# Two raw weight buffers instead of eight, 15 places for split tiles instead of 12, and a newly planned expert stage

## The chip, the cores and the metric

The kernel runs on one core of a Trainium2 chip. The metric is the device time of one execution in microseconds, as the median over runs. Its engines run their own instruction streams and wait for each other through semaphores: PE is the matrix engine (TensorE), ACT the scalar engine, DVE the vector engine, POOL is GpSimd, and SP does nothing but issue DMAs and read registers here. Every time below is from the times of the kernel before or from one profiled execution of it.

## The reference

A causal attention with a window and sink tokens is followed by a mixture of experts, in which each token goes to one expert by the order of its logits, and each expert takes at most 384 tokens.

```python
B, H, S, D = (4, 8, 768, 64); n_sink, window = (4, 128)
keep = is_sink | in_window                       # in_window: 0 <= row - column < 128
a = softmax(where(keep, q @ k.T / sqrt(D), -1e9)); attn = a @ v
x = attn.transpose(0, 2, 1, 3).reshape(B * S, H * D)          # 3072 tokens x 512
N, D, E, F = (3072, 512, 8, 1024)
cap = N // E                                                  # 384
logits = x @ w_gate
for idx in argsort(-logits.flatten()):                        # greedy: the best pairs first
    tok, e = idx // E, idx % E
    if assigned[tok] >= 0 or counts[e] >= cap: continue
    assigned[tok] = e; counts[e] += 1
for e in range(E):
    h = maximum(x[assigned == e] @ w1[e], 0)
    out[assigned == e] = h @ w2[e]
```

All is in float32.

## The kernel before

The attention runs first, in 24 chunks of 128 rows; its result goes to `x_dram` in device memory and the logits stay on chip. The change touches nothing of it.

The experts follow in eight rounds, k = 0 to 7. A round finds by vector work and small matmuls (`phase`, called routing here) the expert that fills up next and its 384 tokens, as the register value `ei` and three columns of row numbers `idx`. The routing of the next round goes on between the matmuls of the round before, on DVE and PE (lines L500 to L672; `cmp` at L500 and L503 are its large comparisons on DVE, `pr` at L519 the matmuls that count them).

A round then has these tasks:

- **Weights** (`weights`). SP reads the expert's number (L676) and issues eight loads of 512 KB (L691): tiles j = 0 to 3 are quarters of `w1`, 4 to 7 quarters of `w2`. A load fills one place of the ring `raw`, which has `NR` places. Each tile is split for exact float32 products: ACT rounds it to `wh` (L693), then DVE takes `wl` as `raw` minus `wh` (L695). `wh` and `wl` are rings of `NW` places. So a load waits until DVE has split the tile that was loaded `NR` loads earlier, and a split waits until PE has read the tile that was split `NW` splits earlier.
- **Rows** (`rows`). POOL issues three gathers of 128 token rows each from `x_dram` into `xg0` to `xg2` (L700). PE transposes them (L708), ACT rounds the result to `xh` (L710) and DVE makes the rest `xl` (L711).
- **Layers** (`mlp`). Layer 1 has eight groups of 12 matmuls into `ph` (L724; for the first two groups of round 0 L721 and L729), after each of which ACT makes `hh` (L731) and DVE `hl` (L732). Layer 2 has three tiles of 24 matmuls into `py` (L740), each of which ACT copies to `yo` (L743) and POOL scatters to the output (L745).

In round 0 the rows are wanted first, and a task named `rowed` on SP holds the loads from j = 2 on (L681): SP reads a word of the tile `xg2`, and so waits until that gather has landed.

Nothing of this order is written by hand. Each task is added to a `Graph` with its engine, a cost, and what it reads and writes; `Graph.order` is a list scheduler that plays the engines forward in time, with a latency for each pair of engines (`ML`), a bias for each class of tasks (`BIAS`), and a window (`WIN`) within which the task of the highest rank is taken though another could start earlier. The program is then emitted in that order on every engine, and each engine executes its instructions in order. The costs decide the order alone, not what an instruction takes on the chip. `run` also puts small matmuls into idle stretches of PE before the first expert matmul (`warm`, L562).

Of the kernel before, what the change touches and what calls it, by code (L numbers as in the profile page):

```python
# [244 lines left out]
def schedule(cfg,off,T,nb=NC,dl={}):
    o=table(cfg); bf=buffers(cfg); WIN=cfg['win']
    rdeps=collections.defaultdict(list); nd={}; ready={}
# [54 lines left out]
    while len(out)<total:  # L302
        best=None
        for e,a in avail.items():
# [67 lines left out]
def plan():  # L372
# [7 lines left out]

RUN=[(4,0)]*2+[(2,2)]*6
STEPS=[(26,64),(20,64),(15,32),(10,32),(5,32),(0,32)]
ML={'VV':127,'EV':200,'EA':220,'VE':300,'AE':260,'AV':142,'VA':130,'AP':180,'PV':180,'PE':215,'VP':180,'PA':180,'PP':60,'AA':35,'EE':0,
    'VS':900,'SD':1500,'VD':1700,'PD':1250,'AD':1700,'ED':1250,'DA':900,'DV':900,'DP':900,'DE':1600,'DD':0,'EP':220,'PQ':1560,}

GWAIT=2000
class Graph:

    def __init__(self): self.t=[]; self.lw={}; self.rd={}
    def add(self,e,cost,fn,r=(),w=(),name='',cls='',lat=None):  # L390
        i=len(self.t); dep={}
# [14 lines left out]
    def order(self,bias,win,free):  # L406
# [12 lines left out]
        while len(out)<n:  # L419
            best=None  # L420
            for e,a in av.items():
# [4 lines left out]
                if e=='D':  # L426
                    W=[(i,max(te,ready[i])) for i in a if T[i][4][0]=='L']; Q=[(ready[i],i) for i in a if T[i][4][0]!='L']
                    i=min(W)[0] if W else None
                    if Q:
                        r,j=min(Q)  # L430
                        if i is None or (max(te,r)<max(te,ready[i]) or max(te,r)==max(te,ready[i]) and max(te,r)>=r+GWAIT-1): i=j
                    x=(0,max(te,ready[i]),i)
# [18 lines left out]
class Moe:  # L451
# [98 lines left out]
    def pools(self,ctx,w1,w2,x_dram,out):  # L550
        tc=self.tc; self.w1,self.w2,self.x_dram,self.out=w1,w2,x_dram,out
        sb=ctx.enter_context(tc.tile_pool(name="fsb",bufs=1)); ps=ctx.enter_context(tc.tile_pool(name="fps",bufs=1,space=PSUM))
        def ring(n,shape,dt,name,p=sb): return [p.tile(shape,dt,name=f"{name}{j}") for j in range(n)]
        self.NR=8; self.raw=ring(self.NR,[128,1024],F32,"raw"); self.NW=12
        self.wh=ring(self.NW,[128,1024],F32R,"wh"); self.wl=ring(self.NW,[128,1024],F32R,"wl")
        self.xg=ring(3,[128,DM],F32,"xg"); self.xh=ring(2,[128,4,CAP],F32R,"xh"); self.xl=ring(2,[128,4,CAP],F32R,"xl")
        self.hh=ring(1,[128,8,CAP],F32R,"hh")[0]; self.hl=ring(1,[128,8,CAP],F32R,"hl")[0]; self.yo=ring(3,[128,DM],F32,"yo")
        self.pt=ring(2,[128,512],F32,"pt",ps); self.ph=ring(3,[128,512],F32,"ph",ps); self.py=ring(2,[128,512],F32,"py",ps); self.pr=ring(1,[128,512],F32,"pr",ps)
        self.nr=0; self.regs={}; self.sc_=[]
# [114 lines left out]
    def weights(self,g,k):  # L674
        nc=self.nc
        def load(): self.regs[k]=nc.sync.value_load(self.ei[k][0:1,0:1],min_val=0,max_val=E-1)  # L676
        g.add('S',100,load,[f'ei{k}'],[f'reg{k}'],f'reg{k}',f'L{k}')
        for j in range(8):
            if k==0 and j==2:

                g.add('S',100,lambda: nc.sync.value_load(self.xg[2][0:1,0:1].bitcast(I32)),['xg2'],['rowed'],'rowed','L0')  # L681
            n=8*k+j; q=n%self.NR; raw=self.raw[q]; s=n%self.NW; wh,wl=self.wh[s],self.wl[s]
            def ld(j=j,raw=raw):
                ei=self.regs[k]
                if j<4:
                    src=self.w1[bass.ds(ei,1),:,256*j:256*j+256].rearrange("o (d p) f -> p (o d) f",p=128)
                    dst=raw.rearrange("p (d f) -> p d f",d=4)
                else:
                    src=self.w2[bass.ds(ei,1),256*(j-4):256*(j-4)+256,:].rearrange("o (f p) d -> p (o f) d",p=128)
                    dst=raw.rearrange("p (f d) -> p f d",f=2)  # L690
                nc.sync.dma_start(dst,src)  # L691
            g.add('D',1450,ld,[f'reg{k}']+(['rowed'] if k==0 and j>1 else []),[f'raw{q}'],f'L{k}.{j}',f'L{k}')
            g.add('A',947,lambda wh=wh,raw=raw: nc.scalar.activation(wh,raw,AF.Copy),[f'raw{q}'],[f'wh{s}'],f'H{k}.{j}',f'W{k}')  # L693
            e='V' if (k,j) in LOV else 'P'
            g.add(e,{'V':1160,'P':2303}[e],lambda wh=wh,wl=wl,raw=raw,e=e: (nc.vector if e=='V' else nc.gpsimd).tensor_tensor(wl,raw,wh.bitcast(F32),OP.subtract),  # L695
                  [f'raw{q}',f'wh{s}'],[f'wl{s}'],f'W{k}.{j}',f'W{k}')
    def rows(self,g,k):
        nc=self.nc; idx=self.idx[k]; b=k%2
        for t in range(3):
            g.add('P',1350,lambda t=t: nc.gpsimd.indirect_dma_start(out=self.xg[t],out_offset=None,in_=self.x_dram,in_offset=bass.IndirectOffsetOnAxis(ap=idx[:,t:t+1],axis=0)),  # L700
                  [f'idx{k}'],[f'xgi{t}',f'xg{t}'],f'G{k}.{t}',f'G{k}')
            g.add('D',1250,None,[f'xgi{t}'],[f'xg{t}'],f'g{k}.{t}',f'G{k}',lat=700)
        for c in range(4):

            tp,tn=(self.py[c%2],f'py{c%2}') if k==0 and c>1 else (self.pt[c%2],f'pt{c%2}')
            pts=[tn,tn+'.1',tn+'.2']
            for t in range(3):
                g.add('E',92,lambda t=t,c=c,tp=tp: nc.tensor.transpose(tp[:,128*t:128*t+128],self.xg[t][:,128*c:128*c+128],self.idn),  # L708
                      [f'xg{t}'],[pts[t]],f'X{k}.{c}.{t}',f'X{k}')
            g.add('A',371,lambda c=c,tp=tp: nc.scalar.activation(self.xh[b][:,c,:],tp[:,0:CAP],AF.Copy),pts,[f'xh{b}.{c}'],f'xh{k}.{c}',f'X{k}')  # L710
            g.add('V',469,lambda c=c,tp=tp: nc.vector.tensor_tensor(self.xl[b][:,c,:],tp[:,0:CAP],self.xh[b][:,c,:].bitcast(F32),OP.subtract),pts+[f'xh{b}.{c}'],[f'xl{b}.{c}'],f'xl{k}.{c}',f'X{k}')  # L711
# [38 lines left out]
    def graph(self):  # L750
        g=Graph()
        for k in range(E):
            self.phase(g,k)
            if k==0: self.rows(g,k); self.weights(g,k); self.mlp(g,k)
            else: self.weights(g,k); self.rows(g,k); self.mlp(g,k)
        return g
    def run(self):
        g=self.graph(); self.g=g
        o=g.order(BIAS,WIN,{})
        self.o=o  # L760
# [11 lines left out]
LOP=[]  # L772
LOV=[(k,j) for k in range(E) for j in range(8) if (k,j) not in LOP]
WARM=[2, 2, 2, 1, 1, 1, 3]
WIN=[0, 666753, 5574]
BIAS={'G0': 6671635, 'G1': 6449503, 'G2': 6705779, 'G3': 8034144, 'G4': 7734947, 'G5': 6407711, 'G6': 6446165, 'G7': 7529680, 'H0': 7140392, 'H1': 6230422, 'H2': 7467794, 'H3': 7341794, 'H4': 8337522, 'H5': 6670993, 'H6': 7528230, 'H7': 8147223, 'L0': 6671635, 'L1': 7366959, 'L2': 8033333, 'L3': 6450452, 'L4': 8157017, 'L5': 7375597, 'L6': 7318303, 'L7': 6494864, 'M0': 7584506, 'M1': 6454307, 'M2': 6446111, 'M3': 5919116, 'M4': 5072608, 'M5': 7410515, 'M6': 7280220, 'M7': 6416193, 'R0': 7765513, 'R1': 8337522, 'R2': 7898561, 'R3': 8766281, 'R4': 7977893, 'R5': 7316483, 'R6': 7567827, 'R7': 7411586, 'T0': 6409393, 'T1': 8034144, 'T2': 6412879, 'T3': 7184173, 'T4': 7399728, 'T5': 7511516, 'T6': 6689144, 'W0': 8310018, 'W1': 7084371, 'W2': 6099157, 'W3': 6473218, 'W4': 6419299, 'W5': 6298013, 'W6': 8117911, 'W7': 6494864, 'X0': 5238855, 'X1': 7198893, 'X2': 6446165, 'X3': 7313265, 'X4': 5911130, 'X5': 5797303, 'X6': 8357941, 'X7': 7271989, 'Y0': 6444567, 'Y1': 7966386, 'Y2': 6670239, 'Y3': 7243724, 'Y4': 8658080, 'Y5': 7230830, 'Y6': 6666651, 'Y7': 7710047}

def attention_general(ctx,tc,qd,kd,vd,iwd,ident,idn,x_dram,L,n_sink,window):

# [91 lines left out]
```

## Time and profile before

| what | value |
|---|---|
| median of 3 runs | 489.02 us (488.76 to 491.45) |
| profiled execution, its own time | 490.33 us |
| its span, first to last instruction | 488.5 us |
| granted TensorE clock, mean | 0.973 |
| attention | 0 to 138.07 us |
| routing and rows of round 0 | 138.07 to 168.69 us |
| expert rounds | 168.69 to 482.50 us |
| PE busy in the expert rounds | 300.72 of 313.81 us |

The time of an execution is about 1.8 us longer than its span. An engine's busy time counts its own work and not the issue of DMAs; what it waited for is taken from the semaphore that came last. "SPq" and "POOLq" are the instruction queues of those engines. L12 is line 12 of the kernel before. In the changed kernel the same lines stand one lower (up to L677) or two lower (L691 is L693, L700 is L702, L740 is L742).

### The profile page before, as it was taken

Reading aid. Unit: us, or ns where it says so; the run is one execution under the profiler, and the core shown is the slowest. Engines: PE = TensorE matmul, PEld = TensorE weight load, DVE = VectorE, ACT = ScalarE, POOL = GpSimd, SP = SyncE. Lnnn points to the kernel's source line nnn. Section 1 sums busy time; section 2 is a strip of 40 time slices with the busy share of each in tenths; the row PEclk is TensorE's granted clock in tenths of the full one; section 3 lists DMA queues with packets and bytes.
Section 4 is the critical chain, followed back from the end, with each engine's and each line's share of the span. In section 5 each row is a group of like instructions: output and inputs, shape, how many; then the busy total and the mean of one; then the engine's idle time right before and its main releaser. Section 6 shows DMA issues by size and latency. Waiting matters only on the chain. (4 is left out here: it accounts for less than half of the span.)

```text
span 488.5 us, 14325 instructions
## 1 busy us (share of the span) xinstructions
PE 442.8 (91%) x5570; PEld 364.5 (75%) x5570; DVE 377.9 (77%) x1167; ACT 226.6 (46%) x667; POOL 171.8 (35%) x322
## 2 busy tenths in 40 slices
PE   8799999999754979989999989989999998999994
PEld 4577777777632668768878868868978877988983
DVE  5899999999956977988987998898898869531210
ACT  4987888888300361541452451262272167332110
POOL 5887878877710300420330230041053023201001
PEclk9999999999965899999999999999999999999998
DMA  8766766753210560930940750571291299301001
GB/s 265 247 222 187 229 217 203 228 171 105 75 43 18 167 228 1 325 148 1 306 147 23 234 215 28 168 264 45 87 323 43 74 355 371 108 0 66 0 22 44
DMA packets 44453, 73.28 MB, mean 150 GB/s; under 512 B 3425, under 2 KB 20961, under 8 KB 44385
## 3 DMA queue, kind: packets, MB, share of 16 engines
q1 hardware_dynamic: 39968, 59.11, 36.5%
q0 software_dynamic: 3840, 12.59, 7.2%
q8 instruction: 44, 0.72, 0.6%
q10 hardware_dynamic: 576, 0.67, 0.5%
q14 instruction: 25, 0.20, 0.1%
HBM read 59.77 MB, written 12.58 MB: 148 GB/s over the span
## 5 line engine op out<-in xcount | busy, mean ns | idle before, releaser
L693 ACT ACTIVATE wh<-raw 128x1024 fp32r<-128x1024 f32 x64 | 67.6, 1060 | 71.6 <-DMA raw<-w 36.7
L700 POOL DMA_INDIRECT xg<-x_dram,idx x24 | 34.7, 1444 | 164.1 <-issue 49.1
L724 PE MATMUL ph<-xh,wh 128*128 128x384 f32 x248 | 87.8, 354 | 0.2 <-DVE hl L732 0.2
L695 DVE TENSOR_TENSOR wl<-raw,wh 128x1024 fp32r<-128x1024 f32 x64 | 77.8, 1219 | 12.1 <-ACT wh L693 11.4
L724 PE MATMUL ph<-xh,wl 128*128 128x384 f32 x248 | 83.7, 337 | 0.0
L724 PE MATMUL ph<-xl,wh 128*128 128x384 f32 x248 | 83.5, 337 | 0.0
L731 ACT ACTIVATE hh<-ph 128x384 fp32r<-128x384 f32 x64 | 31.2, 488 | 106.5 <-PE ph L724 94.4
L740 PE MATMUL py<-wh,hh 128*128 128x512 f32 x192 | 78.6, 409 | 2.2 <-ACT yo L743 1.8
L740 PE MATMUL py<-wh,hl 128*128 128x512 f32 x192 | 75.6, 394 | 1.6 <-DVE hl L732 1.6
L24 ACT ACTIVATE P<-pp,nmx 128x128 f32<-128x128 f32 x192 | 68.7, 381 | 15.7 <-DVE nmx L97 14.7
L740 PE MATMUL py<-wl,hh 128*128 128x512 f32 x192 | 75.3, 392 | 0.0
L745 POOL DMA_INDIRECT out<-yo,idx x24 | 31.9, 1331 | 114.1 <-ACT yo L743 73.6
L732 DVE SCALAR_TENSOR_TENSOR hl<-ph,hh 128x384 fp32r<-128x384 f32 x64 | 35.4, 555 | 27.9 <-ACT hh L731 27.4
L724 PEld LDWEIGHTS ph<-xh,wh 128*128 128x128 f32 x248 | 46.9, 189 | 2.2 <-DVE hl L732 0.6
L724 PEld LDWEIGHTS ph<-xl,wh 128*128 128x128 f32 x248 | 46.7, 188 | 1.7
L724 PEld LDWEIGHTS ph<-xh,wl 128*128 128x128 f32 x248 | 46.6, 188 | 0.0
L83 PE MATMUL pp<-kk,q 64*64 64x204 f32 (+2 forms) x768 | 42.9, 330 | 3.0 <-ACT P L24 1.7
L740 PEld LDWEIGHTS py<-wh,hl 128*128 128x128 f32 x192 | 36.0, 188 | 10.7 <-DVE hl L732 2.8
L740 PEld LDWEIGHTS py<-wh,hh 128*128 128x128 f32 x192 | 36.1, 188 | 9.5 <-ACT yo L743 2.8
L24 ACT ACTIVATION_READ_ACCUMULATOR P<-pp,nmx 128x1 f32 x192 | 41.9, 218 | 0.0
L118 POOL TENSOR_TENSOR E<-PT,me 128x256 f32<-128x256 f32 x48 | 35.4, 755 | 12.5 <-ACT PT L24 12.5
L740 PEld LDWEIGHTS py<-wl,hh 128*128 128x128 f32 x192 | 36.2, 188 | 4.6
(166 smaller groups left out, 799.5 us busy)
## 6 DMA issues: line engine op xcount, KB each, us to landing
raw<-w SPq DMA_DIRECT2D x64, 512.0 KB
kk<-kd SPq DMA_DIRECT2D x23, 272.0 KB
v<-vd SPq DMA_DIRECT2D x24, 256.0 KB
x_dram<-xt SPq DMA_DIRECT2D x24, 256.0 KB
q<-qd SPq DMA_DIRECT2D x22, 256.0 KB
xg<-x_dram,idx POOLq DMA_INDIRECT x24
out<-yo,idx POOLq DMA_INDIRECT x24
us<-ud SPq DMA_DIRECT2D x1, 288.0 KB
```

Source lines behind the costliest of these rows:

```text
L24: def act(*a,**k): last[:]=[nc.scalar.activation(*a,**k)]
L83: PE.matmul(sp[o,s,204*u+a:204*u+204],q[p,2*g+u,o],kk[p,2*i-2+f+a//68:2*i+f+1,2*g+u],start=True,stop=True)
L118: def op_A(c,g): G.tensor_tensor(T('E',c)[:,2*g:2*g+2],diag(c,g),me[:,None].to_broadcast([128,2,2,64]),OP.mult)
L693: g.add('A',947,lambda wh=wh,raw=raw: nc.scalar.activation(wh,raw,AF.Copy),[f'raw{q}'],[f'wh{s}'],f'H{k}.{j}',f'W{k}')
L695: g.add(e,{'V':1160,'P':2303}[e],lambda wh=wh,wl=wl,raw=raw,e=e: (nc.vector if e=='V' else nc.gpsimd).tensor_tensor(wl,raw,wh.bitcast(F32) ...
L700: g.add('P',1350,lambda t=t: nc.gpsimd.indirect_dma_start(out=self.xg[t],out_offset=None,in_=self.x_dram,in_offset=bass.IndirectOffsetOnAx ...
L724: nc.tensor.matmul(p[:,0:CAP],x[:,c,:],y[:,c,:],start=c==0 and i==0,stop=c==3 and i==2)
L731: g.add('A',371,lambda f=f,p=p: nc.scalar.activation(self.hh[:,f,:],p[:,0:CAP],AF.Relu),ps,[f'hh{f}'],f'hh{k}.{f}',f'H{k}')
L732: g.add('V',469,lambda f=f,p=p: nc.vector.scalar_tensor_tensor(self.hl[:,f,:],p[:,0:CAP],0.0,self.hh[:,f,:].bitcast(F32),op0=OP.max,op1=OP ...
L740: nc.tensor.matmul(p,x[:,f,ts],w,start=f==0 and i==0,stop=f==7 and i==2)
L745: st=nc.gpsimd.indirect_dma_start(out=self.out,out_offset=bass.IndirectOffsetOnAxis(ap=idx[:,t:t+1],axis=0),in_=y,in_offset=None)
```

## The change

The raw ring has two places (`NR`), the rings of split tiles 15 (`NW`). A place of any of these rings holds 4 KB of each partition, so the sum is the same: 8 + 2 x 12 = 32 and 2 + 2 x 15 = 32 places. `NRW` is written but read nowhere. SP's hold for `xg2` stands in round 0 before j = 2, as it did, and in round 1 before j = 4; the loads behind it follow by SP's order. In rounds 0 and 1 the graph has the rows ahead of the weights. The other numbers (`ML` for ACT to POOL and DVE to POOL, the cost of a load with j = 1 or 2, that of a gather, `WIN` and `BIAS`) only set the planner's order.

```diff
-ML={...,'AP':180,...,'VP':180,...}
+ML={...,'AP':395,...,'VP':680,...}
+NRW=(2,15)
...
-        self.NR=8; self.raw=ring(self.NR,[128,1024],F32,"raw"); self.NW=12
+        self.NR=2; self.raw=ring(self.NR,[128,1024],F32,"raw"); self.NW=15
...
-            if k==0 and j==2:
-
-                g.add('S',100,lambda: nc.sync.value_load(self.xg[2][0:1,0:1].bitcast(I32)),['xg2'],['rowed'],'rowed','L0')
+            hold=(k,j) in ((0,2),(1,4))
+            if hold:
+
+                g.add('S',100,lambda: nc.sync.value_load(self.xg[2][0:1,0:1].bitcast(I32)),['xg2'],['rowed'],f'rowed{k}.x',f'L{k}')
...
-            g.add('D',1450,ld,[f'reg{k}']+(['rowed'] if k==0 and j>1 else []),[f'raw{q}'],f'L{k}.{j}',f'L{k}')
+            g.add('D',1900 if j in (1,2) else 1450,ld,[f'reg{k}']+(['rowed'] if hold else []),[f'raw{q}'],f'L{k}.{j}',f'L{k}')
...
-            g.add('P',1350,lambda t=t: nc.gpsimd.indirect_dma_start(out=self.xg[t],...),
+            g.add('P',1650 if k<4 else 1200,lambda t=t: nc.gpsimd.indirect_dma_start(out=self.xg[t],...),
...
-            if k==0: self.rows(g,k); self.weights(g,k); self.mlp(g,k)
+            if k<2: self.rows(g,k); self.weights(g,k); self.mlp(g,k)
...
-WIN=[0, 666753, 5574]
-BIAS={'G0': 6671635, 'G1': 6449503, ...}
+WIN=[77, 803571, 2155]
+BIAS={'G0': 9793676, 'G1': 9294495, ...}
```

The program has the same instructions but for two more warm matmuls ahead of the first expert matmul; they stand in another order. Three places show it.

**SP, loads of round 0** (`raw` are the raw places; DMASW0 and DMASW2 are the first and the third gather that POOL has issued, DVE_49 a split on DVE; ISA rows read or set registers). Before:

```order
L691 ISA
L691 DMA raw1_3288<-w1 128x4x256
L691 ISA [waits DMAHW3_49,DMAHW2_49,DMAHW4_49,DMAHW1_49,DMAHW5_49,DMAHW0_49,DMAHW6_49,DMASW2_49,DMAHW7_49,PE_49,Pool_49,Activation_49]
L691 DMA raw2_3289<-w1 128x4x256
L691 ISA
L691 DMA raw3_3290<-w1 128x4x256
L691 ISA
L691 DMA raw4_3291<-w2 128x2x512
```

After:

```order
L693 ISA
L693 DMA raw1_3288<-w1 128x4x256
L693 ISA [waits DMAHW3_49,DMAHW2_49,DMAHW4_49,DMAHW1_49,DMAHW5_49,DMAHW0_49,DMAHW6_49,DMASW0_49,DMAHW7_49,PE_49,Pool_49,Activation_49]
L693 DMA raw0_3287<-w1 128x4x256 [waits DMAHW6_49,DVE_49]
L693 ISA
L693 DMA raw1_3288<-w1 128x4x256 [waits DMAHW7_49,DVE_49]
L693 ISA
L693 DMA raw0_3287<-w2 128x2x512 [waits DMAHW0_49,DVE_49]
```

The hold waited for the third gather and now waits for the first, because POOL gathers `xg2` first in rounds 0 and 1; and each load from j = 2 on now waits for a split.

**DVE, the first splits** (`wl0` to `wl3` are the splits of tiles 0 to 3 of round 0; the others are routing of round 1). Before, at the first and third split:

```order
L531 TENSOR_TENSOR w_105<-w_105,rev_79 128x192
L530 TENSOR_SCALAR f_93<-vm_92 128x24
L695 TENSOR_TENSOR wl0_3307<-raw0_3287,wh0_3295 128x1024
L532 TENSOR_TENSOR s_94<-vm_92,f_93 128x24
L533 TENSOR_REDUCE mx_95<-w_105 128x24
...
L613 TENSOR_REDUCE P1_117<-pr0_3338 128x1
L695 TENSOR_TENSOR wl2_3309<-raw2_3289,wh2_3297 128x1024
L614 TENSOR_TENSOR xb0_103<-x1_102,P1_117 128x24
L595 SCALAR_TENSOR_TENSOR x0_101<-P1_117,y_96 128x24
L503 TENSOR_TENSOR cmp0_109<-xb0_103,grid_66 128x768
```

After, at the same two:

```order
L544 CAST df_108<-di_107 128x120
L697 TENSOR_TENSOR wl0_3304<-raw0_3287,wh0_3289 128x1024
L607 TENSOR_SCALAR odd_113<-pr0_3338 64x8
L697 TENSOR_TENSOR wl1_3305<-raw1_3288,wh1_3290 128x1024
...
L697 TENSOR_TENSOR wl2_3306<-raw0_3287,wh2_3291 128x1024
L614 TENSOR_REDUCE P1_117<-pr0_3338 128x1
L697 TENSOR_TENSOR wl3_3307<-raw1_3288,wh3_3292 128x1024
L615 TENSOR_TENSOR xb0_103<-x1_102,P1_117 128x24
L596 SCALAR_TENSOR_TENSOR x0_101<-P1_117,y_96 128x24
L504 TENSOR_TENSOR cmp0_109<-xb0_103,grid_66 128x768
```

The first split has moved behind the comparison of 128x1536 at L500 (now L501) to the place where the second stood, with the second right behind it. Ahead of the first comparison of 128x768 stand two splits now, `wl2` and `wl3`, where one stood.

**SP, loads of round 1** (DMASW3 is the first gather of round 1). Before:

```order
L691 DMA raw2_3289<-w1 128x4x256 [waits DMAHW0_49,DVE_49]
L691 ISA
L691 DMA raw3_3290<-w1 128x4x256 [waits DMAHW1_49,DVE_49]
L691 ISA
L691 DMA raw4_3291<-w2 128x2x512 [waits DMAHW2_49,DVE_49]
```

After:

```order
L693 DMA raw0_3287<-w1 128x4x256 [waits DMAHW6_49,DVE_49]
L693 ISA [waits DMASW3_49]
L693 DMA raw1_3288<-w1 128x4x256 [waits DMAHW7_49,DVE_49]
L693 ISA
L693 DMA raw0_3287<-w2 128x2x512 [waits DMAHW0_49,DVE_49]
```

Nothing held the loads of round 1 but the splits of round 0; now the fourth load of that round and all behind it wait for its first gather.

## Rows read from the trace of the kernel before

**Rows 1.** The page, part 1: busy time, share of the span, instructions.
```profile
span 488.5 us, 14325 instructions
...
PE 442.8 (91%) x5570; PEld 364.5 (75%) x5570; DVE 377.9 (77%) x1167; ACT 226.6 (46%) x667; POOL 171.8 (35%) x322
```

**Rows 2.** Windows: busy time of each engine in four stretches.
```profile
core 0: us, PE busy (x) PEld busy (x) DVE busy (x) ACT busy (x) POOL busy (x), PEclk, DMA share, GB/s
...
138.07:168.69 30.62, 18.86 (x141) 10.30 (x141) 22.83 (x114) 2.66 (x4) 5.01 (x6) 0.67 0.21 69
168.69:482.50 313.81, 300.72 (x1837) 256.75 (x1837) 231.80 (x673) 120.32 (x181) 61.29 (x44) 1.00 0.41 141
...
210.00:252.00 42.00, 38.47 (x261) 32.31 (x260) 36.88 (x111) 16.36 (x24) 9.10 (x6) 1.00 0.43 147
...
376.00:420.00 44.00, 41.48 (x245) 35.41 (x245) 34.84 (x89) 21.95 (x31) 11.67 (x10) 1.00 0.71 247
```

**Rows 3.** Waits of PE, 168.69 to 482.5 us: total us, times, longest.
```profile
PE pt L708 <- DVE xl L711: 2.3, 2, 1.2
PE pr L519 <- DVE cmp L503: 1.9, 1, 1.9
PE py L740 <- ACT yo L743: 1.8, 4, 0.7
PE py L740 <- DVE hl L732: 1.6, 2, 0.9
PE pr L519 <- DVE cmp L500: 1.4, 2, 1.1
PE pt L708 <- DMA xg<-x_dram,idx: 1.2, 2, 1.0
...
PE py L740 <- ACT hh L731: 0.4, 1, 0.4
```

**Rows 4.** Timeline of SP: start, duration, loads issued in rounds 0 and 1.
```profile
168.46 3.35 SPq L691 DMA_DIRECT2D raw<-w  x6
...
194.74 6.18 SPq L691 DMA_DIRECT2D raw<-w  x8
```

**Rows 5.** Timeline of POOL: first and third gather of round 0, first of round 1.
```profile
160.53 1.17 POOL L700 DMA_INDIRECT xg<-x_dram,idx  x1 [21.60 <-DVE fin L671]
...
163.89 1.59 POOL L700 DMA_INDIRECT xg<-x_dram,idx  x1 [0.31 <-issue]
201.10 1.34 POOL L700 DMA_INDIRECT xg<-x_dram,idx  x1 [35.62 <-PE py L740]
```

**Rows 6.** Timeline of ACT in round 0.
```profile
168.91 0.88 ACT L710 ACTIVATE xh<-py 128x384 fp32r<-128x384 f32 x2
172.46 1.06 ACT L693 ACTIVATE wh<-raw 128x1024 fp32r<-128x1024 f32 x1 [2.67 <-DMA raw<-w]
```

**Rows 7.** Timeline of DVE in round 0: second and third split.
```profile
164.73 1.22 DVE L695 TENSOR_TENSOR wl<-raw,wh 128x1024 fp32r<-128x1024 f32 x1
...
173.56 1.23 DVE L695 TENSOR_TENSOR wl<-raw,wh 128x1024 fp32r<-128x1024 f32 x1 [2.08 <-ACT wh L693]
```

**Rows 8.** Timeline of PE: the first long wait of round 0, one of round 1.
```profile
175.53 0.45 PE L519 MATMUL pr<-oh,cmp 128*128 128x32 bf16 x6 [1.90 <-DVE cmp L503]
...
214.19 0.55 PE L708 MATMUL pt<-idt,xg 128*128 128x128 f32 x3 [1.06 <-DVE xl L711]
```

**Rows 9.** DMA view, 162 to 168 us: busy tenths in 40 slices.
```profile
DMA  0049893795000006951497330000995993200000
```

**Rows 10.** DMA view, 194.7 to 201 us: busy tenths in 40 slices.
```profile
DMA  0004001746799999986973359989998999999999
```

**Rows 11.** DMA view, 202.5 to 205 us: the only queue that moved data.
```profile
DMA packets 543, 0.95 MB, mean 380 GB/s; under 512 B 31, under 2 KB 127, under 8 KB 543
...
q1 hardware_dynamic: 543, 0.95, 105.6%
```

**Rows 12.** Waits of DVE, 168.69 to 420 us: total us, times, longest.
```profile
DVE wl L695 <- ACT wh L693: 10.2, 11, 2.1
```

More of the change, by code (lines that the diff above doesn't have):

```diff
@@ L382 @@
 STEPS=[(26,64),(20,64),(15,32),(10,32),(5,32),(0,32)]
-ML={'VV':127,'EV':200,'EA':220,'VE':300,'AE':260,'AV':142,'VA':130,'AP':180,'PV':180,'PE':215,'VP':180,'PA':180,'PP':60,'AA':35,'EE':0,
+ML={'VV':127,'EV':200,'EA':220,'VE':300,'AE':260,'AV':142,'VA':130,'AP':395,'PV':180,'PE':215,'VP':680,'PA':180,'PP':60,'AA':35,'EE':0,
     'VS':900,'SD':1500,'VD':1700,'PD':1250,'AD':1700,'ED':1250,'DA':900,'DV':900,'DP':900,'DE':1600,'DD':0,'EP':220,'PQ':1560,}
+NRW=(2,15)
 GWAIT=2000
@@ L699, in rows @@
         for t in range(3):
-            g.add('P',1350,lambda t=t: nc.gpsimd.indirect_dma_start(out=self.xg[t],out_offset=None,in_=self.x_dram,in_offset=bass.IndirectOffsetOnAxis(ap=idx[:,t:t+1],axis=0)),
+            g.add('P',1650 if k<4 else 1200,lambda t=t: nc.gpsimd.indirect_dma_start(out=self.xg[t],out_offset=None,in_=self.x_dram,in_offset=bass.IndirectOffsetOnAxis(ap=idx[:,t:t+1],axis=0)),
                   [f'idx{k}'],[f'xgi{t}',f'xg{t}'],f'G{k}.{t}',f'G{k}')
@@ L774 @@
 WARM=[2, 2, 2, 1, 1, 1, 3]
-WIN=[0, 666753, 5574]
-BIAS={'G0': 6671635, 'G1': 6449503, 'G2': 6705779, 'G3': 8034144, 'G4': 7734947, 'G5': 6407711, 'G6': 6446165, 'G7': 7529680, 'H0': 7140392, 'H1': 6230422, 'H2': 7467794, 'H3': 7341794, 'H4': 8337522, 'H5': 6670993, 'H6': 7528230, 'H7': 8147223, 'L0': 6671635, 'L1': 7366959, 'L2': 8033333, 'L3': 6450452, 'L4': 8157017, 'L5': 7375597, 'L6': 7318303, 'L7': 6494864, 'M0': 7584506, 'M1': 6454307, 'M2': 6446111, 'M3': 5919116, 'M4': 5072608, 'M5': 7410515, 'M6': 7280220, 'M7': 6416193, 'R0': 7765513, 'R1': 8337522, 'R2': 7898561, 'R3': 8766281, 'R4': 7977893, 'R5': 7316483, 'R6': 7567827, 'R7': 7411586, 'T0': 6409393, 'T1': 8034144, 'T2': 6412879, 'T3': 7184173, 'T4': 7399728, 'T5': 7511516, 'T6': 6689144, 'W0': 8310018, 'W1': 7084371, 'W2': 6099157, 'W3': 6473218, 'W4': 6419299, 'W5': 6298013, 'W6': 8117911, 'W7': 6494864, 'X0': 5238855, 'X1': 7198893, 'X2': 6446165, 'X3': 7313265, 'X4': 5911130, 'X5': 5797303, 'X6': 8357941, 'X7': 7271989, 'Y0': 6444567, 'Y1': 7966386, 'Y2': 6670239, 'Y3': 7243724, 'Y4': 8658080, 'Y5': 7230830, 'Y6': 6666651, 'Y7': 7710047}
+WIN=[77, 803571, 2155]
+BIAS={'G0': 9793676, 'G1': 9294495, 'G2': 8680892, 'G3': 8986785, 'G4': 10391613, 'G5': 9730842, 'G6': 8800698, 'G7': 8443416, 'H0': 9035735, 'H1': 8707469, 'H2': 7975171, 'H3': 9168980, 'H4': 9176491, 'H5': 10688290, 'H6': 8302192, 'H7': 9060589, 'L0': 8364183, 'L1': 8495933, 'L2': 8069253, 'L3': 9339414, 'L4': 9371499, 'L5': 9801335, 'L6': 8363021, 'L7': 8953574, 'M0': 7938032, 'M1': 9186118, 'M2': 9103865, 'M3': 8685072, 'M4': 8482779, 'M5': 8173316, 'M6': 9342951, 'M7': 8557595, 'R0': 8678968, 'R1': 10940723, 'R2': 10874537, 'R3': 9801479, 'R4': 9349664, 'R5': 8984945, 'R6': 11420537, 'R7': 9070221, 'T0': 9168980, 'T1': 8986785, 'T2': 9149715, 'T3': 8041307, 'T4': 9730842, 'T5': 9371499, 'T6': 8297377, 'W0': 8069253, 'W1': 8686134, 'W2': 8449391, 'W3': 9006870, 'W4': 8379557, 'W5': 9653540, 'W6': 8413001, 'W7': 11306586, 'X0': 8729875, 'X1': 11286798, 'X2': 9793676, 'X3': 11189760, 'X4': 9168980, 'X5': 8985940, 'X6': 8670808, 'X7': 8805083, 'Y0': 8363021, 'Y1': 8678285, 'Y2': 8976736, 'Y3': 8792821, 'Y4': 8743339, 'Y5': 10951003, 'Y6': 10990620, 'Y7': 8744537}
 def attention_general(ctx,tc,qd,kd,vd,iwd,ident,idn,x_dram,L,n_sink,window):
```

## The prediction

> **What bounds the kernel now.** The page's first part comes first: PE is busy 91% of the span and DVE 77% [rows 1]. A mean over stages says little, so the windows come next. In the 30.62 us between the attention and the first expert matmul PE has 18.86 us of work and a granted clock of 0.67 [rows 2]: routing by DVE, then three gathers, which the change reaches only through the order of the last few microseconds. In the 313.81 us of the expert rounds the clock is 1.00 and PE is busy for 300.72 us. PE bounds this stage, and all that a new order of loads can win there is its idle time of 313.81 - 300.72 = 13.1 us.
>
> Where these lie is read from PE's chain of waits [rows 3]. The reader is to see that no wait is for a weight tile: PE waits 2.3 us for `xl`, 1.2 us for gathered rows, 1.9 and 1.4 us for routing comparisons, 1.8 us for `yo`, 1.6 us for `hl`, 0.4 us for `hh`. These are all things that ACT, DVE or a gather deliver late; a burst of loads, followed by a burst of roundings and splits in front of them, can be why. The timelines of SP, ACT and DVE say where it is so.
>
> **Round 0.** The hold lets six loads go at 168.46 us [rows 4], 168.46 - 163.89 = 4.57 us after the third gather began to be issued [rows 5]. ACT then has nothing to round until 172.46 (it waited 2.67 us for the load [rows 6]), so load to rounding takes 172.46 - 168.46 = 4.0 us. DVE stands at the third split for 2.08 us [rows 7], the comparison behind it in DVE's order is late, and PE idles 1.90 us before 175.53 [rows 8].
>
> After the change the hold waits for the first gather, which by the same 4.57 us lands at 160.53 + 4.57 = 165.1. The load also needs the place `raw0`, free when the first split is done. That split now stands where the second stood, which began at 164.73 [rows 7]; with one split of 1.22 us fewer ahead of it and some small instructions more it ends at about 165.0. So the third load goes at 165.1, and the fourth when the second split is done, 1.2 us later at 166.3. They are there at 169.1 and 170.3. ACT is through with `xh` at 168.91 + 0.88 = 169.8 [rows 6], rounds both until 169.8 + 2 x 1.06 = 171.9, and DVE, where now two splits precede the comparison, is through at 171.9 + 1.2 = 173.1 to 173.3, against 173.56 + 1.23 = 174.79 now. The comparison, and PE's start with it, come 1.5 us earlier, inside the 1.90 us of idle time.
>
> The price is that two loads now meet the second and third gather, on which the first expert matmul waits. One load at 380 GB/s [rows 11] takes 0.524 / 0.380 = 1.4 us; that is the upper bound, the third gather standing behind one load, and 0 the lower. In the later burst the engines are full about 1.5 us after the first load is issued (the tenth slice of 0.16 us [rows 10]), so a load issued at 165.1 has its data moving from about 166.6, while the gathers' data end at about 167.1 (slice 34 of 0.15 us [rows 9]). I take the overlap, 0.4. Round 0 gives -1.5 + 0.4 = **-1.1** (from -1.9, all the wait, to +1.4). The layer 2 tiles of round 0 come one by one instead of in a burst; layer 1, until about 195, hides this, so I cost it at nothing.
>
> **Rows of round 1.** Eight loads are issued over 6.18 us from 194.74 [rows 4], and the first gather follows at 201.10 [rows 5]. Between 202.5 and 205 us the hardware queue of the loads alone moves data, with all engines full [rows 11], though that gather has been issued. The rows are late and PE idles 1.2 us for them and 1.06 us for `xl` at 214.19 [rows 3, 8]: 2.3 us. With two raw places at most two loads stand ahead of a gather, and the fourth load waits for the first. I take all of it, **-2.3**. The lower bound is 0. The upper one is -3.5, the 1.2 and the whole 2.3 of `xl`, as the rest of `xl` lies in a later round with the same pattern.
>
> On this the Trainium skill has a rule, "DMA: Bandwidth & Descriptors", section Queues, rings and completion order: each DMA engine takes turns between the queue rows that have work, a packet at a time. By it a gather would not stand behind queued loads. The trace does not show it in those 2.5 us [rows 11], perhaps because the gather had no data to move yet; it makes a rival below.
>
> **The other waits behind bursts.** `yo` 1.8, `hl` 1.6, the comparison at L500 1.4 and `hh` 0.4 make 5.2 us [rows 3]. With loads paced by splits, roundings can no longer come as a burst of eight. No row shows how many of these waits are due to that; DVE is busy for 36.88 of 42.00 us in a typical stretch [rows 2] and would be late now and then anyway. Bounds 0 and -5.2; I take half, **-2.6**.
>
> **The new wait.** Six of eight loads in each round used to find a raw place free for long; now each load from the third on waits for a split two loads earlier. First the rate: a place is taken from the load's issue to the end of its split, 4.0 us to the rounding and 174.79 - 172.46 = 2.3 us for rounding and split [rows 6, 7], 6.3 us. Two places give a tile every 3.2 us, eight in 25 us, and a round lasts 313.81 / 8 = 39.2 us. So the rate doesn't bind. What can bind is order: ACT and DVE execute in order, and a rounding or split whose load isn't there blocks what stands behind it, `hh`, `yo` and `xh` on ACT, `hl`, `xl` and routing on DVE, which PE waits for. And a split that is late behind routing makes the load two later late. Today DVE waits 10.2 us at splits [rows 12], and three waits of PE are of the kind that follow such a stand, 1.9 + 1.4 + 1.6 = 4.9 us [rows 3], about half. Lower bound 0: the plan leaves each load time, and 15 instead of 12 split places let splits run three tiles further ahead. Upper bound: one stand more like the 2.08 us [rows 7] in each of rounds 1 to 6, 12.5 us, half of which reaches PE, 6.2. From the lower side I take DVE's waits to grow by half, 5.1, and half of that at PE, **+2.5**.
>
> Two more warm matmuls lie in idle time of PE ahead of the first expert matmul; nothing. SP's extra hold in round 1 delays loads that have layer 1's eight groups to arrive; nothing, and where that cover goes it is the new wait.
>
> **Sum**: -1.1 - 2.3 - 2.6 + 2.5 = -3.5. The profiled execution took 490.33 us, so 486.8 by it; it stood 1.3 us over the median of 489.02, and by the median the forecast is 485.5 us. The ends of all terms give -1.9 - 3.5 - 5.2 = -10.6 and 1.4 + 6.2 = +7.6.
>
> **Rivals**, all by the median.
>
> *Slower: the splits starve.* Place: DVE's splits in rounds 1 to 6, each with a load that could not be issued in time. Price: +6.2 for it, the 5.2 us of waits stay, as ACT and DVE stand again, and round 0 wins nothing; -2.3 + 6.2 = +3.9, 492.9 us. It decides from 2.3 + 2.4 = 4.7 us of new waits at PE, 2.4 us being the half per cent below. For it: DVE is 88% busy where it matters [rows 2], so a late split finds no slack. Against: the rate, 25 of 39.2 us.
>
> A sentence of the Trainium skill stands beside it: "Perfetto Trace Analysis", section Optimization Strategy, says that the same gap, repeated, can mean too few buffers for the next tile. The trace before, with eight raw places, shows no wait of PE for a weight tile; by the page fewer places would bring such gaps back, at each round.
>
> *Same: the idle time moves on.* PE waits for DVE because DVE is busy 88% there, and what PE gains in one place it loses at the next comparison: net about nothing, 489.0. For it: 1.9 + 1.4 + 1.6 us of PE's waits are on DVE's own work. Against: those of round 0 and of the gathers end with a DMA.
>
> *Same: gathers don't stand behind loads.* Engines serve the gathers' queue in turn, the rows of round 1 were late for their late issue alone, and the term of 2.3 falls away: -1.2, 487.8. The Trainium skill's section on arbitration, named above, would have it so.
>
> *Same: the holds do little.* They wait for one gather only; the loads then collide with the other two. Round 0 gives -1.5 + 1.4, round 1 nothing: -0.1 - 2.6 + 2.5 = -0.2, 488.8.
>
> *Larger gain.* No new wait, and all the waits behind bursts go: -1.1 - 2.3 - 5.2 = -8.6, 480.4. Against: DVE's load.
>
> **How the numbers follow.** A difference of 0.5% (2.4 us) is about what a measurement of this kernel can tell from none. Forecast 0.46, with a range of its own of 482.0 to 486.5; larger gain 0.08; idle moves on 0.13; gathers served in turn 0.08; holds do little 0.06; splits starve 0.19. Faster: 0.46 + 0.08 = 0.54; same: 0.13 + 0.08 + 0.06 = 0.27; slower 0.19. The range of 481.0 to 492.0 leaves out about half of the larger gain and a little over half of the starving splits, some 0.15.
>
> **What would show it.** Right: the wait of 1.90 us at the comparison of 128x768 in round 0 is gone or under 0.5 us, and the first expert matmul starts within 0.7 us of 168.69; the waits for `xg` and `xl` in round 1 fall from 2.3 to under 0.5 us; ACT's roundings lie apart by 3 us or more instead of in runs; PE idles 9 to 10 us in the expert rounds instead of 13.1. Wrong: DVE's waits at splits go from 10.2 to over 20 us, or PE waits for `wl` or `wh` at all; the first expert matmul starts after 170; or a stretch of the rounds loses clock, which stands at 1.00 now and which none of my terms holds.

## The result and the profile after

The changed kernel takes 482.98 us (482.87 to 483.4, 3 runs) against 489.02: a ratio of 0.9886 with the interval 0.9843 to 0.9928, so 6.0 us faster. A later comparison of the same two kernels gave 483.49 against 489.12 us and 0.9892 (0.9846 to 0.9939).

The stage first. This is the window of the expert rounds (columns as in [rows 2]), from the first expert matmul to the last:

```profile
171.28:474.50 303.22, 299.18 (x1837) 257.62 (x1837) 232.97 (x673) 119.93 (x180) 55.15 (x44) 1.00 0.45 144
```

The rounds took 313.1 us (168.69 to 481.8) and take 303.2, 9.9 less, and PE is idle for 4.0 us of them, not 12.4. (The 13.1 us of the prediction count 0.7 us behind the last expert matmul, as the window of [rows 2] ends at 482.50.) PE's waits there, to set beside [rows 3]:

```profile
PE pr L612 <- DVE i L608: 2.3, 5, 0.8
PE pt L710 <- DVE xl L713: 0.5, 1, 0.5
PE pr L520 <- DVE cmp L501: 0.3, 1, 0.3
PE ph L723 <- ACT xh L712: 0.3, 1, 0.3
PE pr L520 <- DVE R L655: 0.2, 1, 0.2
```

They were 12.1 us and are 3.6. All waits for `yo`, `hl`, `hh`, for gathered rows and for the smaller comparison are gone. Only the wait for a routing step (L607, now L608) has grown, from 1.0 to 2.3 us, and one of 0.2 us for `R` is new.

POOL's timeline has the gathers (to set beside [rows 5]):

```profile
162.32 1.17 POOL L702 DMA_INDIRECT xg<-x_dram,idx  x1 [21.72 <-DMA raw<-w]
...
198.77 0.94 POOL L702 DMA_INDIRECT xg<-x_dram,idx  x1 [32.69 <-PE py L742]
```

The first gather of round 1 was issued 201.10 - 168.69 = 32.4 us after the first expert matmul and now 198.77 - 171.28 = 27.5 us after it. Round 0 on DVE, the splits `wl2` and `wl3` and the comparison behind them ([rows 7] has the former third split):

```profile
173.53 1.22 DVE L697 TENSOR_TENSOR wl<-raw,wh 128x1024 fp32r<-128x1024 f32 x1
174.67 0.16 DVE L614 TENSOR_REDUCE P<-pr 128x1 f32<-128x8 f32 x1
174.83 1.22 DVE L697 TENSOR_TENSOR wl<-raw,wh 128x1024 fp32r<-128x1024 f32 x1
...
176.18 0.56 DVE L504 TENSOR_TENSOR cmp<-xb,grid 128x768 bf16<-128x768 bf16 x1
```

No wait of DVE stands there any more, and the comparison follows the first expert matmul by 176.18 - 171.28 = 4.90 us, not by 174.91 - 168.69 = 6.22. From the first gather to the first expert matmul it takes 171.28 - 162.32 = 8.96 us, against 8.16.

DVE's waits at splits up to 420 us (beside [rows 12]):

```profile
DVE wl L697 <- ACT wh L695: 9.1, 16, 1.5
```

Over the whole of the rounds, first before, then after:

```profile
DVE wl L695 <- ACT wh L693: 11.4, 14, 2.1
```

```profile
DVE wl L697 <- ACT wh L695: 19.5, 22, 3.7
```

So DVE stands at splits longer than before, by 8.1 us, but the growth lies behind 420 us, where PE has no wait at all.

### The profile page after: what moved, and what is told of

The parts are those of the page before. It is cut to its first block, busy times and chain, and to the rows that moved or that the text cites. A ratio compares the mean times of both kernels' runs of the same rounds, so it can differ in the third digit from the quotient of the medians.

```text
span 481.2 us, 14324 instructions
## 1 busy us (share of the span) xinstructions
PE 441.7 (92%) x5572; PEld 365.9 (76%) x5572; DVE 381.3 (79%) x1167; ACT 227.3 (47%) x667; POOL 163.7 (34%) x322
## 4 chain that ended last, share of the span: by engine, by line
PE 46%; DVE 31%; DMA 8%; issue 6%; ACT 6%; POOL 2%; POOLq 0%; SPq 0%; DVEq 0%; ACTq 0%
PE ph L726 17%; PE py L742 15%; DMA raw<-w 7%; DVE wl L697 5%; DVE nmx L95 3%; ACT P L24 3%; DVE cmp L501 3%; PE pp L83 3%; PE pr L520 2%; PE ph L563 2%; PE pp L132 2%; DVE pp L89 2%; ACT wh L695 2%; DVE xl L713 1%; DVE at L139 1%
## 5 line engine op out<-in xcount | busy, mean ns | idle before, releaser
L697 DVE TENSOR_TENSOR wl<-raw,wh 128x1024 fp32r<-128x1024 f32 x64 | 78.1, 1221 | 19.6 <-ACT wh L695 19.5
L702 POOL DMA_INDIRECT xg<-x_dram,idx x24 | 29.9, 1247 | 146.9 <-PE py L742 52.0
L747 POOL DMA_INDIRECT out<-yo,idx x24 | 29.4, 1223 | 129.6 <-ACT yo L745 103.4
```

The costliest lines, as they stand in the source:

```text
L702: g.add('P',1650 if k<4 else 1200,lambda t=t: nc.gpsimd.indirect_dma_start(out=self.xg[t],out_offset=None,in_=self.x_dram,in_offset=bass.I ...
L747: st=nc.gpsimd.indirect_dma_start(out=self.out,out_offset=bass.IndirectOffsetOnAxis(ap=idx[:,t:t+1],axis=0),in_=y,in_offset=None)
```

## Experiments

The change has three parts that experiments can separate: the order of each engine's instructions, the sizes of the rings, and the holds. So that a ring can be changed and not the order, `run` was given two settings: the planner orders the graph of one (`PLAN`), and the tasks are emitted, each engine's in that order, with the rings and holds of the other (`EMIT`). With both the same, the program is that of the changed kernel, or of the one before. In these kernels lines stand one lower again (L702 is L703).

```diff
-        g=self.graph(); self.g=g
-        o=g.order(BIAS,WIN,{})
-        self.o=o
+        self.cfg=PLAN; g=self.graph(); o=g.order(BIAS,WIN,{})
+        self.cfg=EMIT; h=self.graph(); self.g=h; self.o=o
...
```

Each ratio is to the kernel before as it ran in the same comparison (488.7 to 490.3 us); PE's waits are those from the first expert matmul to the last.

| run | order planned for | raw, split places | us | ratio to before (interval) | PE's waits in the rounds, for rows |
|---|---|---|---|---|---|
| before | before | 8, 12 | 489.0 | 1 | 12.1, 1.2 |
| changed, again | change | 2, 15 | 483.49 | 0.9892 (0.9846 to 0.9939) | 4.5, 0 |
| old_raw2 | before | 2, 12 | 572.28 | 1.1664 (1.1611 to 1.1717) | 68.2, 0 |
| new_8_12 | change | 8, 12 | 488.76 | 0.9989 (0.9953 to 1.0025) | 7.0, 6.2 |
| new_4_14 | change | 4, 14 | 481.45 | 0.9865 (0.982 to 0.9909) | 3.3, 1.0 |
| new_4_14, again | change | 4, 14 | 481.82 | 0.9852 (0.9815 to 0.9889) | 1.8, 0.4 |
| new_2_12 | change | 2, 12 | 484.55 | 0.9876 (0.9833 to 0.9919) | 6.2, 0 |
| new_nohold1 | change | 2, 15 | 483.4 | 0.9881 (0.983 to 0.9932) | 5.3, 0 |
| new_8_12_holds | change | 8, 12 | 487.94 | 0.9988 (0.9956 to 1.0021) | 6.2, 4.9 |
| new_8_12_holdlast | change | 8, 12 | 494.51 | 1.01 (1.0062 to 1.0139) | 12.2, 0 |
| new_h0last | see below | 2, 15 | 483.25 | 0.9903 (0.9873 to 0.9934) | 4.5, 0 |
| replan_old_2_15 | its own, old numbers | 2, 15 | 500.06 | 1.0219 (1.0165 to 1.0273) | 14.0, 0 |
| replan_new_8_12 | its own, new numbers | 8, 12 | 496.04 | 1.0137 (1.0098 to 1.0175) | 10.7, 0.8 |

### Order and rings crossed: old_raw2 and new_8_12

```diff
 old_raw2, EMIT against the kernel before
-NR=8
+NR=2
 new_8_12, EMIT against the changed kernel
-NR=2, NW=15
+NR=8, NW=12
```

> Order of every engine as in the kernel before, instruction for instruction; only the raw ring is cut from eight places to two (12 split places stay). Theory A (the loads: fewer raw places pace them, bursts of loads no longer delay gathers and fill ACT and DVE): faster than before by 2 to 5 us, 484 to 487 us, with the waits of PE for gathered rows in round 1 (1.2 and 1.06 us) gone. Theory B (the order: where splits, routing and hl stand on DVE decides, and the two raw places only suit an order that spreads the splits): in the order of before the splits stand in runs, each of which would now wait for a load that waits for the split two earlier; same or slower, 489 to 495 us, with DVE's waits at splits well over 20 us and PE's waits over 12 us.

> Order of every engine as in the changed kernel, instruction for instruction, both holds too; the rings are those of before, eight raw places and 12 split places. Theory A (the loads): the loads come in bursts again, gathers stand behind them and most of the gain is lost, 486 to 489 us. Theory B (the order): the splits stay spread on DVE whatever the loads do, loads only come earlier, so the gain stays, 482.5 to 484.5 us, PE's waits in the expert rounds stay under 5 us.

Two raw places with the order of before cost 82 us (572.28 against 490.25 in the same comparison), far more than theory B gave. PE's waits in its rounds:

```profile
PE pr L521 <- DVE cmp L502: 16.9, 5, 7.0
PE py L743 <- ACT yo L746: 16.2, 6, 6.0
PE pr L613 <- DVE i L609: 15.1, 5, 5.2
PE ph L727 <- DVE hl L735: 8.7, 2, 7.4
```

These are the waits of before, many times as long (`yo` 16.2 us instead of 1.8, the large comparison 16.9 instead of 1.4). DVE's waits at splits were 11.4 us; in old_raw2:

```profile
DVE wl L698 <- ACT wh L696: 77.4, 35, 6.1
```

The split that is next on DVE, or the rounding that is next on ACT, has no load yet, and routing, `hl` and `yo` stand behind it. The starving splits of the prediction are real; the order decides on them.

With the order of the change and eight raw places the time is that of before within the interval, which reaches 2.3 us of gain. PE's waits:

```profile
PE pt L711 <- DMA xg<-x_dram,idx: 6.2, 5, 1.8
PE pr L521 <- DVE cmp L502: 0.3, 1, 0.3
PE ph L724 <- ACT xh L713: 0.3, 1, 0.3
PE pr L521 <- DVE R L656: 0.2, 1, 0.2
```

Of the waits on DVE and ACT 0.8 us are left, where the kernel before has 10.9. So these go by the order, with loads in bursts or not; whether the places of the splits or those of the routing do it, no run separates. What is new is that PE waits 6.2 us for gathered rows instead of 1.2. Together its waits are 5.1 us shorter than before, and the rounds take 307.2 us instead of 313.1, while the medians (488.76 and 490.25) lie only 1.5 us apart. Why the time shows so little of it stays open; the rounds of the kernel before are known from one execution alone. Part 6 of the profile's page has the median from a gather's issue to its landing, first with eight raw places, then (the changed kernel) with two:

```profile
xg<-x_dram,idx POOLq DMA_INDIRECT x24, 6.5
```

```profile
xg<-x_dram,idx POOLq DMA_INDIRECT x24, 4.1
```

The first gather of round 2 in new_8_12 was issued at 237.57 us, in 0.99 us. The DMA view has the queues in 238.6 to 242.1 us and in 242 to 243 us (packets, MB, share of 16 engines; q0 is the queue of the gathers, q1 that of the loads):

```profile
q1 hardware_dynamic: 802, 1.29, 103.3%
...
q0 software_dynamic: 4, 0.02, 1.2%
...
q0 software_dynamic: 57, 0.23, 60.0%
q1 hardware_dynamic: 87, 0.16, 45.3%
```

For 3.5 us the loads move nearly all the data, then the two queues share the engines about evenly. In the changed kernel the same gather was issued at 236.79 us, in 0.99 us too, and no load moved data beside it; from 237.8 to 240.1 us:

```profile
q0 software_dynamic: 80, 0.26, 45.2%
```

All its 0.26 MB were moved in that time. Neither theory had the whole: order and rings are both needed, and each for its own waits.

### The number of raw places: new_4_14, and new_2_12

> Order of the changed kernel, four raw places and 14 split places, both holds as in it. Theory A: up to four loads can be queued ahead of a gather instead of two or eight, so PE's waits for gathered rows lie between 0 (two places) and 6.2 us (eight), about 1 to 2.5 us, and the time is 483.5 to 486 us. Theory B (two places are special): as with eight places, 487 to 489 us.

> Order of the changed kernel, two raw places, but 12 split places instead of 15. If the 15 places give something (splits that run ahead of PE's reads by more than 12 tiles): DVE's and ACT's roundings wait for PE at the end of a layer, 484 to 487 us. If the order alone counts, and it needs no more than 12: 483 us, within 0.5 us of the changed kernel. In the changed kernel's trace 21 splits have begun when layer 1 of round 2 starts and 12 when that of round 1 does, at most 5 tiles into the round at hand, which speaks for the second.

The waits for rows go 0, 1.0 (0.4 when run again) and 6.2 us with two, four and eight places, and the gathers land after 4.1, 4.6 and 6.5 us: theory A for the waits, in their size too. The time, at least as short as with two places, lies below the range that theory A gave. Twelve split places instead of 15 change nothing that can be measured: 484.55 us lies in the range of the first expectation, but the kernel before took 490.25 in that comparison, and the ratio of 0.9876 is no worse than the changed kernel's. The larger split rings are no part of the gain that shows here; they use the room that the raw ring freed.

### The hold of round 1: new_nohold1

> The changed kernel with the second hold taken out: SP no longer waits for the first gather of round 1 ahead of the load with j = 3; all else in the same order. Theory A: with two raw places at most two loads can stand ahead of the gathers anyway, so 483 to 484 us; if the hold does carry the gain of round 1, PE waits for the rows there again, up to 2.3 us, 485 us. Theory B: no change, 483 us. By the trace the load after the hold was issued at 204.15 us, when its raw place came free at 204.13, so the hold should have been over by then.

0.9881 against 0.9886, and PE waits for no rows: the hold carries nothing that shows. By the expectation's figures its load could not go earlier anyway, as its place came free at 204.13 us.

### Holding the loads for the gathers with eight places: new_8_12_holds and new_8_12_holdlast

> Order of the changed kernel with rings of 8 and 12, as in new_8_12, and beside the hold of round 0 one in each round 1 to 7 ahead of the load with j = 3, which waits for the last gather of that round. In new_8_12 PE waited 6.2 us in the expert rounds for gathered rows and for nearly nothing else; the gathers landed 6.5 us after their issue against 4.1. Theory A (two raw places help because few loads are queued ahead of the gathers): with at most three loads ahead the gathers land after 4 to 5 us, PE's waits for rows fall from 6.2 to under 1.5 us and the time to 482.5 to 485.5 us; what is left may go to splits whose load is now late, 0 to 2 us. Theory B (the raw ring matters in another way, such as the pace of ACT or the load on the DMA engines as a whole): the waits for rows move but the time stays at 487 to 489 us.

This run missed its aim. In rounds 2 to 7 the graph has the weights ahead of the rows, and there the hold read the `xg2` of the round before; in round 1 the planner moved the tile that the hold names to the front of the gathers. It is new_8_12 over again, and its 487.94 us a second reading of that (488.76). The next kernel has the rows first in every round and the hold's tile changed in `EMIT` alone.

```diff
+hold before j=3 in rounds 1 to 7
-['xg2']
+['xg1'] in round 1, ['xg2'] in the others: gathered last
```

> Order of the changed kernel on PE, DVE, ACT and POOL, rings of 8 and 12 as in new_8_12, and on SP a hold in each round 1 to 7 ahead of the load with j = 3 that does wait for the last gather of that round (in new_8_12_holds it stood behind the first gather in round 1, and in rounds 2 to 7 read the tile of the round before). Theory A (few raw places help because few loads are queued ahead of a gather): gathers land 4 to 5 us after their issue instead of 6.5, PE's waits for rows fall from 6.2 to under 1.5 us, and the time from 488.8 to between 482.5 and 486 us; the load with j = 3 is up to 2.5 us late for its split in rounds 1 and 3, which may leave PE 0 to 3 us of waits on DVE. Theory B (the raw ring matters otherwise): 487 to 489 us, whatever becomes of the gathers.

Half of theory A came out: the gathers land after 3.8 us and PE waits for no rows. The time did not: 494.51 us. PE's waits:

```profile
PE pr L613 <- DVE i L609: 7.7, 3, 6.8
PE py L743 <- ACT yo L746: 2.1, 1, 2.1
```

The 6.8 us come from a split of round 5. DVE's timeline there:

```profile
361.28 0.17 DVE L608 TENSOR_SCALAR odd<-pr 64x8 f32<-64x8 f32 x1
368.21 1.23 DVE L698 TENSOR_TENSOR wl<-raw,wh 128x1024 fp32r<-128x1024 f32 x1 [6.77 <-ACT wh L696]
369.47 0.16 DVE L609 SCALAR_TENSOR_TENSOR i<-pr,odd 64x8 bf16<-64x8 f32 x1
```

The held load is late for a split that stands early in the order, and the routing step behind it keeps PE. This hold exchanges the wait for rows for a stand at a split. Two or four raw places avoid both with this order (PE's waits are 1.8 to 6.2 us): each load goes as soon as there is a place, and few ever queue.

### The planner's own order: replan_old_2_15 and replan_new_8_12

```diff
 replan_old_2_15, against the kernel before
-self.NR=8 ... self.NW=12
+self.NR=2 ... self.NW=15
 replan_new_8_12, against the changed kernel
-self.NR=2 ... self.NW=15
+self.NR=8 ... self.NW=12
```

> The kernel before with the rings of the change (2 raw places, 15 split places) and nothing else: the planner makes its own order for them with its old numbers (costs, latencies, window, bias, rows ahead of the weights in round 0 alone, hold in round 0 alone). In the order of before two raw places cost 81 us; here the order knows of them. Theory A (rings and pacing carry the gain, any order that is planned for two places serves): 483 to 487 us. Theory B (the new numbers, by which splits, routing and hl stand where they do on DVE, carry it): 488 to 500 us, with PE's waits on DVE and ACT at 10 us or more.

> The changed kernel with the rings of before, 8 and 12, and everything else of the change; the planner makes its own order with the new numbers. With eight raw places the plan puts the splits of a round into runs again (those of round 0 stand 2 to 8 instructions apart on DVE, in the changed kernel 2 to 18). Theory A with B (the gain has two parts: splits spread out on DVE because the plan knows of two places, and few loads ahead of the gathers): both are gone, 487 to 493 us, with PE's waits in the expert rounds at 8 us or more. If the new numbers carry the gain by themselves: 482.5 to 485 us.

Both are slower than before. Planned for two places with the old numbers, the splits are spread (from the first to the last of round 1 it is 53 instructions of DVE; 37 before, 59 in the changed kernel), but PE waits 5.5 us for the large comparison and 4.9 us for the step at L609, which suggests that the routing stands badly between them. Planned for eight places with the new numbers the splits bunch again (37) and PE's first waits are

```profile
PE pr L521 <- DVE cmp L502: 3.8, 4, 3.2
PE pr L613 <- DVE i L609: 3.6, 3, 2.8
PE py L743 <- ACT yo L746: 1.2, 1, 1.2
```

and its first expert matmul comes 12.5 us after the first gather instead of 9.0. The rings without the numbers lose 11 us, the numbers without the rings 7, both together gain 6. Which of the new numbers counts (bias, window, the two latencies, the costs, the rows ahead in round 1) was not tried.

### A tile renamed, and the best version: new_h0last, changed_again, new_4_14_again

> The changed kernel with both holds waiting for xg1, the third gather of rounds 0 and 1, instead of xg2, the first. In the changed kernel the first expert matmul came 8.96 us after the first gather was issued, against 8.16 before; if that is the price of the two loads that meet the later gathers, it comes 0.5 to 0.8 us earlier again here. The third split then is late by up to 3 us, and PE waits 0 to 2 us for the comparison behind it in round 0, as before. Sum between -0.8 and +1.5 us: 482 to 484.5 us.

This missed its aim too: the planner gathered `xg1` first in both rounds, so the hold waits for the first gather as before and only names differ. It serves as a repetition: 0.9903, with the first matmul 8.3 us after the first gather. Over the kernels with the change's order and two places this stretch was 8.3 to 9.2 us.

> The changed kernel, unaltered, for a comparison on the same chip as new_4_14_again: ratio to before 0.985 to 0.992. Its expert rounds in the trace at 302 to 306 us, of which PE waits 3 to 5 us.

> The changed kernel's order with four raw and 14 split places once more, on the same chip as the changed kernel. If its 481.5 us against 483 was chance: within 1 us of the changed kernel. If four places are better, because a load need not wait for a split two earlier while at most four stand ahead of a gather: 1 to 2 us under the changed kernel.

Four raw and 14 split places took 481.45 and 481.82 us, the changed kernel 482.98, 483.49; the intervals overlap, but both readings are 1.5 to 1.7 us lower, and in the second one PE's waits are down to 1.8 us. It is the fastest version here; that it beats the changed kernel is likely, not shown.

## Why the prediction held

The forecast was 485.5 us, range 481.0 to 492.0, faster with 0.54; the result lies 2.5 us below it, in the likeliest case's own range of 482.0 to 486.5. By its steps, from the waits of PE:

- **Round 0**, -1.1 = -1.5 + 0.4: the first part is right. With the loads held for the first gather and not for the third, the third split runs without a wait, and PE's wait of 1.90 us at the comparison is gone. The second part isn't shown: PE waits for no gathered rows ahead of the first expert matmul. That the stretch before it is 0.8 us longer, so that -1.9 + 0.8 gives -1.1 again, is luck; its cause is below.
- **Rows of round 1**, -2.3: 2.3 to 0.5, -1.8 (1.2 us are left when run again, all for `xl`). The size was about right and the cause half so. That gathers stand behind queued loads is shown by new_8_12. But they were also issued 4.9 us earlier after the first matmul, and this the prediction didn't see. It comes with the order: in new_8_12 it is 27.1 us after the first expert matmul, and PE still waits 1.21 us for rows of round 1, so the earlier issue alone doesn't do it.
- **The other waits behind bursts**, -2.6 as half of 5.2: 0.3 us are left, -4.9. Mis-sized, and the cause was the wrong one: not bursts of loads but the order on DVE and ACT, as new_8_12 has none of these waits but 0.3 us, with loads in bursts. The diffs of the order ahead of the prediction showed the start of it.
- **The new wait**, +2.5: this is the step that failed. Up to 420 us DVE's waits at splits were to grow by half, from 10.2 us; they fell to 9.1 and the longest from 2.1 to 1.5. Over the whole rounds they did grow, from 11.4 to 19.5 us, but not half of the growth reached PE: of its waits on DVE the routing step's grew by 1.3 us, all before 420 us. The bound of +6.2 was far too low where the order doesn't fit (82 us) and too high where it does.
- **What no middle value held**: 1.2 us for `xl` in round 6 went too (the upper bound for rows had it), and PE's busy time fell by 1.5 us, 300.72 to 299.18.

Waits -8.5 and busy time -1.5 make, but for rounding, the 9.9 us of the rounds. Against that the first matmul came 2.6 us later in this profiled execution: 1.7 because its attention, which is the same program, ended later, and 0.8 by the stretch from the first gather on. So 490.33 became 482.87 us, -7.5 in the profiled executions, and -6.0 in the medians. The end of the attention is POOL's last instruction of it, first before, then after:

```profile
138.73 0.20 POOL L153 TENSOR_TENSOR L<-xt 128x8 f32<-128x8 f32 x1
```

```profile
140.39 0.20 POOL L153 TENSOR_TENSOR L<-xt 128x8 f32<-128x8 f32 x1
```

The stretch is filled by PE itself. In the changed kernel 25 warm matmuls stand ahead of the first rows; with the same order and rings new_h0last took 1.3 us less for them. First the changed kernel, then new_h0last, each with its window from the first gather to the first expert matmul:

```profile
160.45 6.74 PE L563 MATMUL ph<-grid,onesb 128*128 128x384 bf16 x25
...
162.32:171.28 8.96, 8.71 (x58) 5.43 (x56) 7.59 (x29) 2.66 (x4) 3.15 (x3) 0.82 0.67 179
```

```profile
159.53 5.43 PE L564 MATMUL ph<-grid,onesb 128*128 128x384 bf16 x25
...
161.40:169.71 8.31, 7.57 (x59) 5.00 (x57) 7.51 (x29) 2.66 (x4) 3.15 (x3) 0.96 0.70 199
```

PE is busy for 8.71 of the 8.96 us, at a granted clock of 0.82 instead of 0.96. So 0.65 of the 0.8 us come with the lower clock, in this execution and not in the other, and are no price of the loads. The prediction put the warm matmuls at nothing, as idle time of PE.

In the rounds alone its terms gave -1.5 - 2.3 - 2.6 + 2.5 = -3.9 us, and PE's waits fell by 8.5. That the middle of the forecast is off by only 2.5 us is therefore partly luck: the rounds gained over twice what it said, and the medians show 6.0 us. Of its own signs, the wait of 1.90 us is gone and the rows of round 1 are at 0.5 us. But the first expert matmul came at 171.28, which it had named as a sign of being wrong, ACT's roundings still come in pairs (172.24 and 173.74 us in round 0) and not 3 us apart, and PE idles 4.0 us and not 9 to 10. None of the other signs of being wrong came: the granted clock of the rounds is 1.00, and PE never waits for `wl` or `wh`.

Of the rivals, the starving splits came true in old_raw2, and the one by which gathers don't stand behind loads did not: in new_8_12 they wait. On this the Trainium skill's rule, "DMA: Bandwidth & Descriptors", section Queues, rings and completion order, that engines take turns between the queue rows that have work, agrees with the even shares of 242 to 243 us. It doesn't tell the 3.5 us before, in which the gather had been issued and moved almost nothing; whether its queue had work for the engines then, the trace doesn't show. The other rule weighed, that of the Trainium skill, "Perfetto Trace Analysis", section Optimization Strategy, that a repeated gap can mean too few buffers, agrees with old_raw2 (68.2 us of waits) and not with the changed kernel (3.6): the number of places is too small or not only for a given order.

## What to carry to other kernels

When instructions execute in order, a wait that is in nobody's way in one order stops an engine in another. A smaller ring has no price of its own, it has one with an order: two places instead of eight cost 82 us with one order here and gained about 5 with another (new_8_12 against the changed kernel). To tell order and ring apart, keep the order and change the ring, and the other way round. And a deep ring for loads isn't free: eight loads in a queue delayed a small transfer on which the next stage waited, and two to four places were deep enough here.

## What the runs showed of the hardware that was not expected

PE's clock after a long wait. In new_8_12_holdlast PE idles 6.83 us before 369.68. The windows of the stretch before, the idle time and the time behind it (columns as in [rows 2]; the granted clock stands behind POOL):

```profile
358.00:362.80 4.80, 4.80 (x32) 3.62 (x33) 3.34 (x7) 0.50 (x1) 3.23 (x4) 1.00 0.56 163
362.80:369.70 6.90, 0.07 (x2) 0.01 (x1) 1.38 (x2) 1.06 (x1) 0.00 (x0) 0.88 0.76 245
369.70:374.00 4.30, 4.30 (x19) 3.19 (x19) 1.95 (x9) 0.44 (x2) 0.00 (x0) 0.50 0.73 279
374.00:378.00 4.00, 4.00 (x27) 3.14 (x26) 3.25 (x9) 3.25 (x7) 0.00 (x0) 0.90 0.00 0
```

The clock falls from its upper level to the lower, 0.50, and a matmul into `py` takes 0.63 to 0.78 us there, instead of 0.39 to 0.48 behind it:

```profile
369.68 0.17 PE L613 MATMUL pr<-i,wt 128*128 128x8 bf16 x1 [6.83 <-DVE i L609]
...
370.28 0.63 PE L743 MATMUL py<-wl,hh 128*128 128x512 f32 x1
...
375.07 0.40 PE L743 MATMUL py<-wl,hh 128*128 128x512 f32 x1
```

In the profiled execution of old_raw2 (578.12 us) the granted clock of the rounds is 0.89 and PE's busy time 326.80 us instead of 300.72: of the 81.5 us by which its rounds are longer, 26 are the same work done slower. The clock is as low in its other executions, 0.90 to 0.92 over the whole span, against 0.96 to 0.98 for the kernel before.

The attention, the same instructions in all kernels, ended at different times. POOL's last instruction of it in new_nohold1 and in new_2_12:

```profile
137.02 0.20 POOL L153 TENSOR_TENSOR L<-xt 128x8 f32<-128x8 f32 x1
```

```profile
143.11 0.20 POOL L153 TENSOR_TENSOR L<-xt 128x8 f32<-128x8 f32 x1
```

Six microseconds lie between them, as much as the whole effect. What causes it stays open; profiled executions are therefore best compared by the rounds alone.
